# Row maxima of two early stages sent through ScalarE's own DMA queue, and a new order of the first pairs of an attention kernel

## The chip, the cores and the metric

The kernel runs on one core of one Trainium2 chip. The metric is the device time of one execution in microseconds (us), the median over several runs. TensorE is called PE, VectorE DVE, ScalarE ACT, GpSimd POOL and SyncE SP, as in the profile. SP here does nothing but issue DMAs. L531 is line 531 of the kernel.

## The reference: what is computed

Causal attention with a decay bias, four batches of eight heads, 576 positions, 64 dimensions, then two feed-forward layers on the 2304 tokens:

```python
scores = scale * np.matmul(q, k.transpose(0, 1, 3, 2))
cum = np.cumsum(np.maximum(s, 0.0), axis=-1)
bias = -(cum[:, :, :, None] - cum[:, :, None, :])
scores = np.where(causal, -1000000000.0, scores + np.minimum(bias, 0.0))
scores = scores - np.max(scores, axis=-1, keepdims=True)
attn = np.exp(scores)
attn = attn / (np.sum(attn, axis=-1, keepdims=True) + 1e-09)
out = np.matmul(attn, v)
# layer 1
h = x @ w_in
x = (h - np.tanh(h)) @ w_out
# layer 2
h = x @ w_in
x = (h * np.clip(h + 3.0, 0.0, 6.0) / 6.0) @ w_out
```

## The kernel before

**Tiling.** The 32 heads are worked as 16 pairs; all of the attention comes first (until about 185 us), then the two layers, which are long runs of matmuls and are not touched by the change. Pair 0 is split into its two heads, each with its own loads, row maxima and rows; every other pair is one unit.

**The steps of a pair p**, by the names that the planner uses (the line is that of the kernel before):
- `lq`, `lk` load q and k (L490, 288 KB each for a pair); `q1` and `k2` are copies by ACT (L466, L480), `kh` a cast by DVE (L477), `q2` a DMA from one q tile to another (`Q<-Q`, through `move`, L279), `ql` and `kl` subtractions by POOL (L474, L484), `cu` a DMA of the running sums of s.
- `mx`: PE multiplies q and k for the row maxima (L531); `rd`: DVE reduces the products (L540).
- `mf`: DVE scales, splits and transposes the maxima (L569 to L576). `mo` sends the rows to DRAM (`mdram<-xr`, 16 KB) and `mi` brings them back as two rows of the q tile (`Q<-mdram`): one round trip, two DMAs in series, both issued by SP through `move`.
- `st`: PE computes the scores in four tiles (L633), of which one operand contains the two rows that `mi` brings; `ex`: ACT's exponentials (L636); `pv`: the values and the sums (L666, L677) with v loaded by `lv` (L598); `ov`: copies out by ACT (L701).

So the scores of a head can start only when its maxima have come back from DRAM, and the planner puts the maxima of the next pairs (`mx`) between them. Where PE has nothing ready early on, **fillers** are put in (`zeros()`, L1354): matmuls of zeros into an idle PSUM bank. `FILLS` names the operation in front of which they stand and how many microseconds of them, counted at 0.115 us each. 18 wide ones (L1369) open the program.

**What sets the order.** A list-scheduling planner (`Plan`) gives every operation a planned start from the durations and due times that the code passes to it. The instructions of each engine stand in the order of these starts, and every engine runs its own in that order. `PRIO` is a table of offsets of the due times, one for each kind of step; `MOVES` then moves single operations behind others by hand. A DMA stands in the order of the engine that issues it. `first_mf` and `first_mo` list the operations `mf` and `mo` in the order head 0, head 1, pair 1, pair 2 ..., so that `first_mo[:1]` is the `mo` of the first head; operations in an `after` list wait for them in the plan alone.

`scores(h, hh, ...)` takes its rows from `omi[x]`, the `mi` of its own head or pair.

Of the kernel before, what the change touches and what calls it, by code (L numbers as in the profile page):

```python
# [23 lines left out]
NPR = NH // 2  # L24
# [6 lines left out]
ON = {}  # L31
MOVES = [("cu0b", 0, "cu0", 0), ("q2_0", 1, "lk1", 0), ("kh1", 0, "rd1_0", 0), ("mf0", 1, "rd1_2", 0)]
FILLS = {"mx1_0": 0.9, "mx2_1": 3.0, "st0_0": 0.9, "mx4_1": 2.4, "st1_0": 0.5, "pv1_3": 1.5}
NS1, NS2, NIN = 4, 2, 3
# [33 lines left out]
UMX = ((0, 1, 2, 3, 4, 5), (4, 0, 1, 3, 2))  # L68
KDMA = ()
TINY, HUGE = (float(np.array([b], np.uint32).view(np.float32)[0]) for b in (0x38000000, 0x47F00000))  # L70

# [8 lines left out]
PRIO = {  # L80
# [3 lines left out]
}  # L84
# [46 lines left out]
class Plan:  # L131
# [18 lines left out]

    def dma(self, fn, kb, after=(), bufs=(), prio=0.0, name="", n=1):
        return self.op("SP", n * self.ISSUE, fn, after, bufs, prio, kb, name)

# [6 lines left out]
    def schedule(self):  # L160
# [12 lines left out]
        while done < len(self.ops):  # L173
# [14 lines left out]
            while again:  # L188
                again = False
                for e in ready:  # L190
# [35 lines left out]
                    if e == "SP":  # L226
                        dma_free = max(dma_free, t + o.dur) + o.kb / self.DMA_KB_US
                        o.end = dma_free + self.DMA_US
                    else:
                        o.end = t + o.dur + self.LAT[e]  # L230
                    heapq.heappush(events, free[e])
# [28 lines left out]
def kernel(  # L260
# [14 lines left out]
    def f32(a):  # L275
        return a.bitcast(F32)

    def move(dst, src):
        nc.sync.dma_start(f32(dst), f32(src))  # L279

# [35 lines left out]
    def r(b):  # L316
        return late[b.t] if isinstance(b.t, str) else b.t
# [124 lines left out]
    alloc_prev = [None, None]  # L442
    first_mf, first_mo = [], []
    filled = []
# [5 lines left out]
    def heads(p):  # L450
# [10 lines left out]
        for i, a in enumerate(parts):  # L461
# [26 lines left out]
            def ld(x, a=a):  # L488
# [3 lines left out]
            lq, lk = (plan.dma(  # L492
                lambda x=x, ld=ld: ld(x), 147 * n, [cm] if p == 1 else first_mo[:1] if p == 2 else first_mo[1:2] if p else [], [tq], t + PRIO["lq"], name=f"l{'qk'[x]}{p}"
            ) for x in range(2))
# [4 lines left out]
            else:  # L499
              okh.append(plan.op("DVE", vec_us(n * S, 1.92, 150), kh, [lk, al], [b1, tq], t + PRIO["kh"], name=f"kh{p}", port=True))  # L500
              ok2.append(plan.op("ACT", act, k2, [lk, a2], [b2, tq], early(t + PRIO["k2"], 1.05), name=f"k2_{p}"))
            oq2.append(plan.dma(q2, 147 * n, [oq1[-1], a2], [b1, b2], t + PRIO["q2"], name=f"q2_{p}"))
            oql.append(plan.op("POOL", pool, ql, [oq1[-1], a2] + first_mf[: 2 * (p == 1)], [b1, b2, tq], early(t + PRIO["ql"], 2), name=f"ql{p}", port=True))
# [59 lines left out]
        for i, a in enumerate(parts):  # L563
            n = a.stop - a.start
            mr = Buf(mrp)

            def mf(a=a, n=n, mr=mr):
                if n == 2:
                    nc.vector.tensor_copy(r(mt)[0:D, 1, 4:5], r(mt)[D:P, 0, 4:5])  # L569
                m = r(mt)[:, a]  # L570
                hi, lo = (r(MT)[:, x * 5 * n : (x + 1) * 5 * n].rearrange("p (a i) -> p a i", a=n) for x in range(2))
                nc.vector.tensor_scalar_mul(hi, m, -1.0)  # L572
                nc.vector.scalar_tensor_tensor(
                    out=lo, in0=m, scalar=-1.0, in1=f32(hi), op0=ALU.mult, op1=ALU.subtract
                )
                return nc.vector.transpose(f32(r(mr)), f32(r(MT)))  # L576

            def mo(i=i, mr=mr):
                move(mdram[p if i == 0 else NPR], r(mr))

            def mi(a=a, i=i, n=n):
                rows = mdram[p if i == 0 else NPR].rearrange("(b n) r -> n b r", b=4)[0 : 10 * n]
                rows = rows.rearrange("(j n) b r -> j n b r", j=2)
                if n == 2:
                    dst = r(b1)[0][66:68].rearrange("j a (i b r) -> j (a i) b r", i=5, b=4)
                else:
                    dst = r(b1)[0][66:68, a.start].rearrange("j (i b r) -> j i b r", i=5, b=4)
                move(dst, rows)

            dep = sum((mm_mx[hh] for hh in range(a.start, a.stop)), [])  # L590
            u = t0 + PRIO["mf"] if p else lead + a.start
            omf = plan.op("DVE", 0.55 + 0.1 * n, mf, dep, [mt, MT, mr], u, name=f"mf{p}", port=True)
            omo = plan.dma(mo, 16, [omf], [mr], u, name=f"mo{p}")
            first_mo.append(omo)
            first_mf.append(omf)
            omi.append(plan.dma(mi, 5, [omo], [b1], u, name=f"mi{p}"))

        lv = plan.dma(lambda: nc.sync.dma_start(r(vf).rearrange("p j a d -> p (j a d)"), v[p]), 338, first_mo[1:2] if p else first_mo[:1], [vf], t0 + PRIO["lv"], name=f"lv{p}")  # L598
        k2s.append(ok2[-1])
# [835 lines left out]
```

## Time and profile before

| what | value |
|---|---|
| median of 3 runs | 945.47 us (944.84 to 946.5) |
| the profiled execution's own time | 944.47 us |
| its span (first to last instruction) | 942.7 us |
| mean clock granted to TensorE over the span | 0.998 of full |
| busy: PE, DVE, ACT, POOL | 931.3, 662.9, 467.3, 159.3 us |

The span is cut short of the execution's own time by 1.8 us of start and end. An engine is busy when one of its instructions runs; PE's busy time does not tell fillers from work, nor a slow clock from a fast one. A row of a timeline gives the start, the busy time of a run of equal instructions, the engine, the line, the tiles (destination, arrow, sources) and the count; in square brackets stands the idle time before it, with the work that ended it.

### The profile page before, as it was taken

To read this page: it belongs to the slowest core of one execution; us is meant where nothing else is said; L and a number is where in the kernel's file an instruction comes from. 1 tells how busy PE (TensorE), PEld (TensorE's weight loads), DVE (VectorE), ACT (ScalarE), POOL (GpSimd) and SP (SyncE) were. 2 spreads that over 40 slices of the span, in tenths; PEclk is the share of its full clock that TensorE was granted. 3 is DMA by queue.
4 is the path that set the end of the run, shared out by engine and by line. 5 is a ranking of instruction groups with operands and counts; after the bars stand their busy time and mean duration, and the time that the engine had idled before them with its cause. 6 is when DMAs were issued, how large, how long until landed. Compare 5 with 4: busy or idle time off the path is not lost.

```text
span 942.7 us, 18003 instructions
## 1 busy us (share of the span) xinstructions
PE 931.3 (99%) x7112; PEld 839.0 (89%) x7112; DVE 662.9 (70%) x1059; ACT 467.3 (50%) x720; POOL 159.3 (17%) x113
## 2 busy tenths in 40 slices
PE   8999999999999999999999999999999999999998
PEld 5888888788788889988888888999999999999997
DVE  7798897889985776676577641848767477674763
ACT  7577777655443444444344333544545344454441
POOL 7446756500000000022332321000000000000000
PEclk9999999999999999999999999999999999999999
DMA  5666876777235445564546862766887668776762
GB/s 156 170 180 176 235 197 182 229 286 233 89 121 220 179 185 217 202 202 156 216 153 223 262 218 78 261 214 222 267 276 242 212 221 267 274 245 216 223 223 92
DMA packets 69793, 193.75 MB, mean 206 GB/s; under 512 B 11856, under 2 KB 20656, under 8 KB 68428
## 3 DMA queue, kind: packets, MB, share of 16 engines
q1 hardware_dynamic: 69708, 192.59, 63.0%
q8 instruction: 56, 0.92, 0.4%
q14 instruction: 29, 0.24, 0.1%
HBM read 143.74 MB, written 44.09 MB: 199 GB/s over the span
## 4 chain that ended last, share of the span: by engine, by line
PE 91%; DVE 5%; POOL 1%; DMA 1%; issue 1%; ACT 1%; SPq 0%; DVEq 0%; POOLq 0%; ACTq 0%
PE bank L903 21%; PE bank L934 20%; PE pair L1271 19%; PE pair L1195 18%; PE bank L633 5%; PE bank L666 3%; DVE xr L540 2%; PE bank L677 2%; PE bank L531 1%; PE wide L531 1%; DMA Q<-Q 1%; PE bank L1354 1%; DVE xr L572 1%; DVE K L477 0%; POOL K L484 0%
## 5 line engine op out<-in xcount | busy, mean ns | idle before, releaser
L934 PE MATMUL bank<-gg,w 128*128 128x512 f32 (+1 forms) x960 | 234.4, 368 | 0.5 <-ACT gg L922 0.5
L903 PE MATMUL bank<-xx,w 128*128 128x512 f32 (+1 forms) x960 | 233.4, 368 | 0.0
L934 PEld LDWEIGHTS bank<-gg,w 128*128 128x128 f32 x960 | 170.4, 188 | 30.6 <-ACT gg L922 0.9
L903 PEld LDWEIGHTS bank<-xx,w 128*128 128x128 f32 x960 | 170.4, 189 | 30.2 <-issue 0.2
L1195 PE MATMUL pair<-op_w,w 128*128 128x384 f32 x648 | 117.9, 335 | 0.2
L1195 PEld LDWEIGHTS pair<-op_w,w 128*128 128x128 f32 x648 | 112.4, 188 | 1.2 <-DVE g L918 0.6
L914 ACT ACTIVATE g<-bank 128x512 f32<-128x512 f32 (+1 forms) x80 | 44.4, 555 | 136.9 <-PE bank L903 66.3
L924 POOL TENSOR_TENSOR gg<-g,gg 128x512 fp32r<-128x512 f32 x32 | 48.3, 1510 | 343.8 <-ACT gg L922 246.6
L918 DVE TENSOR_TENSOR g<-bank,g 128x512 f32<-128x512 f32 (+1 forms) x80 | 50.9, 636 | 73.5 <-ACT g L914 72.6
L1271 PE MATMUL pair<-w,op_W 128*128 128x256 f32 x774 | 97.8, 283 | 0.0
L1271 PEld LDWEIGHTS pair<-w,op_W 128*128 128x128 f32 x774 | 95.4, 192 | 0.0
L922 ACT ACTIVATE gg<-g 128x512 fp32r<-128x512 f32 (+1 forms) x80 | 47.0, 588 | 49.4 <-DVE g L918 27.4
L633 PE MATMUL bank<-Q,K 128*128 128x320 f32 (+9 forms) x384 | 65.8, 313 | 1.8 <-DMA Q<-Q 0.9
L636 ACT ACTIVATE pt<-bank 128x512 f32<-128x512 f32 (+2 forms) x128 | 59.1, 508 | 17.1 <-PE bank L633 12.0
L633 PEld LDWEIGHTS bank<-Q,K 128*128 128x128 f32 (+3 forms) x384 | 56.2, 186 | 8.1 <-issue 2.5
L1271 PE MATMUL pair<-w,op_B 128*128 128x256 f32 x486 | 62.7, 283 | 0.0
L1271 PEld LDWEIGHTS pair<-w,op_B 128*128 128x128 f32 x486 | 60.5, 192 | 0.0
L540 DVE CUSTOM_DVE_ANT_0 xr<-bank,xr 128x512 bf16<-128x512 f32 (+3 forms) x96 | 49.0, 510 | 14.5 <-PE bank L531 3.8
L474 POOL TENSOR_TENSOR Q<-tq,Q 64x1152 fp32r<-64x1152 f32 (+1 forms) x17 | 43.0, 2530 | 46.5 <-PE bank L531 22.2
L666 PE MATMUL bank<-pt,vf 128*32 128x192 f32 (+3 forms) x1152 | 46.7, 315 | 0.0
L484 POOL TENSOR_TENSOR K<-tq,K 64x1152 fp32r<-64x1152 f32 (+1 forms) x17 | 42.8, 2522 | 10.9 <-ACT Q L468 3.7
L666 PEld LDWEIGHTS bank<-pt,vf 128*32 128x32 f32 x1152 | 32.1, 110 | 11.0 <-DVE xr L540 0.6
(322 smaller groups left out, 1347.2 us busy)
## 6 DMA issues: line engine op xcount, KB each, us to landing
w<-wdram SPq DMA_DIRECT2D x149, 512.0 KB
wdram<-cv SPq DMA_DIRECT2D x56, 512.0 KB
raw_c<-in_w_dram SPq DMA_DIRECT2D x11, 1024.0 KB
raw_b<-in_w_dram SPq DMA_DIRECT2D x11, 1024.0 KB
raw_a<-in_w_dram SPq DMA_DIRECT2D x12, 512.0 KB
vf<-in_v_dram SPq DMA_DIRECT2D x16, 330.0 KB
rb<-rdram SPq DMA_DIRECT2D x32, 144.0 KB
xdram<-xb SPq DMA_DIRECT2D x16, 288.0 KB
```

What stands on the lines that cost most here:

```text
L540: nc.vector.tensor_tensor_reduce(out=junk[0:rr, 0:w], in0=r(b)[0:rr, col : col + w], in1=maskB[:, 0:w] if hh < 0 else maskA[0:rr, m0 : m0 ...
L633: nc.tensor.matmul(o, w, x, start=(i == 0), stop=(i == len(mms) - 1), skip_group_check=True)
L636: nc.scalar.activation(r(pt), r(b)[:, 0 : CW[c]], AF.Exp, scale=0.125)
L666: nc.tensor.matmul(r((wide_b, rest_b)[far])[32 * i : 32 * i + 32, oc : oc + n], r(vf)[:, j, hh, d0 : d0 + 32], r(pts[hh][c])[:, col : col ...
L903: nc.tensor.matmul(r(ps)[:, 0:w], wt[:, c, :], x(c)[:, 0:w], start=(part == 0 and c == 0), stop=(part == 2 and c == NCC - 1),)
L914: nc.scalar.activation(r(g)[:, 0:w], r(ps)[:, 0:w], AF.Tanh)
L918: nc.vector.tensor_sub(x, r(ps)[:, 0:w], x)
L922: gho = plan.op("ACT", vec_us(w, 1.2, 205), lambda: nc.scalar.activation(r(gh)[:, 0:w], r(g)[:, 0:w], AF.Copy), [m, to_gg], [g, gh], base)
L924: glo = plan.op("DVE" if beside else "POOL", vec_us(w, 0.96, 155) if beside else vec_us(w, 0.44, 160), lambda: (nc.vector if beside else n ...
L934: nc.tensor.matmul(r(acc[e])[:, 0:w], a[:, es], bb[:, 0:w], start=f, stop=l)
L1195: nc.tensor.matmul(bank(k)[:, l], w[hw][:, l, kc], r(x)[:, hx, kc], start=(i in (1, 5, 2) and j == 0 and kc == 0), stop=(j == 2 and kc == ...
L1271: nc.tensor.matmul(r(c[k])[:, m * 256 : (m + 1) * 256], r(x)[:, hx, l, m * P : (m + 1) * P], w[hw][:, l], start=(i == order[chain_first[k] ...
```

## The change

It does five things.
- `OWNQ = (1,)`: for the second head of pair 0 and for pair 1, `mo` and `mi` are issued by ACT (`nc.scalar`) in a DMA queue of its own, and not by SP. These are four DMAs.
- The planner counts a DMA issued by ACT with the landing time of a DMA.
- The loads of pair 2 (the third pair) get a due time near the start (`lead + 2`), in front of `q2_1` (`lead + 5`) and of `lv0` (`lead + 3`); `q2_1` also stands after the first head's `mo`, and the loads of the later pairs and of v wait, in the plan, for an `mf` and no longer for an `mo`.
- The table `PRIO` is new, which orders the steps of all pairs anew, and `MOVES` has two more entries, which put `mi` of the second head behind that head's exponential 1 of the first head (`ex0_1`) and `q1` of pair 2 behind `ex0_3`.
- `FILLS`: the fillers in front of pair 1's maxima (`mx2_1`) go from 3.0 to 4.4 us, those in front of the first scores go, those in front of the second head's scores go from 0.5 to 0.6, those in front of pair 2's maxima go from 2.4 to 1.2, and those in front of the first values go.

```diff
--- before.py
+++ after.py
@@ -29,8 +29,10 @@
 NEG = -8.0e9
 WARM = 18
 ON = {}
-MOVES = [("cu0b", 0, "cu0", 0), ("q2_0", 1, "lk1", 0), ("kh1", 0, "rd1_0", 0), ("mf0", 1, "rd1_2", 0)]
-FILLS = {"mx1_0": 0.9, "mx2_1": 3.0, "st0_0": 0.9, "mx4_1": 2.4, "st1_0": 0.5, "pv1_3": 1.5}
+MOVES = [
+    ("cu0b", 0, "cu0", 0), ("q2_0", 1, "lk1", 0), ("kh1", 0, "rd1_0", 0), ("mf0", 1, "rd1_2", 0), ("mi0", 1, "ex0_1", 0), ("q1_2", 0, "ex0_3", 0),
+]
+FILLS = {"mx1_0": 0.9, "mx2_1": 4.4, "st1_0": 0.6, "mx4_1": 1.2}
 NS1, NS2, NIN = 4, 2, 3
 NPT = (3, 3, 3, 3)
 PVG = ((0, 1, 2, 3),)
@@ -67,6 +69,7 @@
 ]
 UMX = ((0, 1, 2, 3, 4, 5), (4, 0, 1, 3, 2))
 KDMA = ()
+OWNQ = (1,)
 TINY, HUGE = (float(np.array([b], np.uint32).view(np.float32)[0]) for b in (0x38000000, 0x47F00000))
 
 BLOCKS = [(0, t0, w) for t0, w in ((0, 512), (512, 512), (1024, 256), (1280, 512), (1792, 512))]
@@ -78,9 +81,9 @@
 
 
 PRIO = {
-    "lq": -83.65, "q1": 73.45, "kh": -32.51, "k2": -25.57, "q2": 94.58, "ql": -115.49, "kl": 41.37, "cu": 56.98, "mx": -24.12, "rd": 29.37,
-    "mf": -136.78, "mo": -203.04, "mi": -117.08, "lv": -137.83, "st": 6.08, "ex": -106.35, "pv": 17.91, "ov": -39.21, "sd": 23.64, "so": -123.9,
-    "no": 107.64, "conv": 202.63, "T": 6.478, "dst": 0.344, "sp": 27.42, "dsp": 24.45,
+    "lq": 39.12, "q1": 73.45, "kh": -91.19, "k2": 105.65, "q2": -6.45, "ql": -64.52, "kl": 41.37, "cu": -137.68, "mx": -24.12, "rd": 129.89,
+    "mf": -136.78, "mo": 59.8, "mi": -126.96, "lv": -137.83, "st": 5.7, "ex": -84.37, "pv": 12.68, "ov": 141.74, "sd": 103.06, "so": -123.9,
+    "no": 84.45, "conv": 198.97, "T": 6.478, "dst": 0.344, "sp": 27.42, "dsp": -52.34,
 }
 
 
@@ -148,8 +151,8 @@
         self.ops.append(o)
         return o
 
-    def dma(self, fn, kb, after=(), bufs=(), prio=0.0, name="", n=1):
-        return self.op("SP", n * self.ISSUE, fn, after, bufs, prio, kb, name)
+    def dma(self, fn, kb, after=(), bufs=(), prio=0.0, name="", n=1, own=False):
+        return self.op("ACT" if own else "SP", n * self.ISSUE, fn, after, bufs, prio, kb, name)
 
     @staticmethod
     def later(ready, free, e, item, t):
@@ -227,7 +230,7 @@
                         dma_free = max(dma_free, t + o.dur) + o.kb / self.DMA_KB_US
                         o.end = dma_free + self.DMA_US
                     else:
-                        o.end = t + o.dur + self.LAT[e]
+                        o.end = t + o.dur + (self.DMA_US if o.kb else self.LAT[e])
                     heapq.heappush(events, free[e])
                     heapq.heappush(events, o.end)
                     done += 1
@@ -275,8 +278,8 @@
     def f32(a):
         return a.bitcast(F32)
 
-    def move(dst, src):
-        nc.sync.dma_start(f32(dst), f32(src))
+    def move(dst, src, own=False):
+        (nc.scalar if own else nc.sync).dma_start(f32(dst), f32(src))
 
     keep = ctx.enter_context(tc.tile_pool(name="keep", bufs=1))
     dram = ctx.enter_context(tc.tile_pool(name="dram", bufs=1, space=bass.MemoryType.DRAM))
@@ -440,7 +443,7 @@
 
     T = PRIO["T"]
     alloc_prev = [None, None]
-    first_mf, first_mo = [], []
+    first_mf, first_mo, first_mi = [], [], []
     filled = []
     st_done, pv_done, prep_done, ov_done, rd_done = {}, [], [], {}, []
     batch_sd, batch_ov, norm_ops = {}, {}, {}
@@ -490,7 +493,7 @@
                 nc.sync.dma_start(dst, (q, k)[x][p][:, a.start * S : a.stop * S])
 
             lq, lk = (plan.dma(
-                lambda x=x, ld=ld: ld(x), 147 * n, [cm] if p == 1 else first_mo[:1] if p == 2 else first_mo[1:2] if p else [], [tq], t + PRIO["lq"], name=f"l{'qk'[x]}{p}"
+                lambda x=x, ld=ld: ld(x), 147 * n, [cm] if p == 1 else first_mo[:1] if p == 2 else first_mf[1:2] if p else [], [tq], lead + 2 if p == 2 else t + PRIO["lq"], name=f"l{'qk'[x]}{p}"
             ) for x in range(2))
             oq1.append(plan.op("ACT", act + 0.22 * (p > 0), q1, [lq, al], [b1, tq], early(t + PRIO["q1"], 1), name=f"q1_{p}"))
             if p in KDMA:
@@ -499,7 +502,7 @@
             else:
               okh.append(plan.op("DVE", vec_us(n * S, 1.92, 150), kh, [lk, al], [b1, tq], t + PRIO["kh"], name=f"kh{p}", port=True))
               ok2.append(plan.op("ACT", act, k2, [lk, a2], [b2, tq], early(t + PRIO["k2"], 1.05), name=f"k2_{p}"))
-            oq2.append(plan.dma(q2, 147 * n, [oq1[-1], a2], [b1, b2], t + PRIO["q2"], name=f"q2_{p}"))
+            oq2.append(plan.dma(q2, 147 * n, [oq1[-1], a2] + first_mo[:1] * (p == 1), [b1, b2], lead + 5 if p == 1 else t + PRIO["q2"], name=f"q2_{p}"))
             oql.append(plan.op("POOL", pool, ql, [oq1[-1], a2] + first_mf[: 2 * (p == 1)], [b1, b2, tq], early(t + PRIO["ql"], 2), name=f"ql{p}", port=True))
             okl.append(plan.op("POOL", pool, kl, [ok2[-1]] + first_mf[: 2 * (p == 1)], [b2, tq], t + PRIO["kl"] if p else lead + 3.5 + 0.1 * i, name=f"kl{p}", port=True))
 
@@ -575,27 +578,30 @@
                 )
                 return nc.vector.transpose(f32(r(mr)), f32(r(MT)))
 
-            def mo(i=i, mr=mr):
-                move(mdram[p if i == 0 else NPR], r(mr))
-
-            def mi(a=a, i=i, n=n):
+            own = p + i in OWNQ
+
+            def mo(i=i, mr=mr, own=own):
+                move(mdram[p if i == 0 else NPR], r(mr), own)
+
+            def mi(a=a, i=i, n=n, own=own):
                 rows = mdram[p if i == 0 else NPR].rearrange("(b n) r -> n b r", b=4)[0 : 10 * n]
                 rows = rows.rearrange("(j n) b r -> j n b r", j=2)
                 if n == 2:
                     dst = r(b1)[0][66:68].rearrange("j a (i b r) -> j (a i) b r", i=5, b=4)
                 else:
                     dst = r(b1)[0][66:68, a.start].rearrange("j (i b r) -> j i b r", i=5, b=4)
-                move(dst, rows)
+                move(dst, rows, own)
 
             dep = sum((mm_mx[hh] for hh in range(a.start, a.stop)), [])
             u = t0 + PRIO["mf"] if p else lead + a.start
             omf = plan.op("DVE", 0.55 + 0.1 * n, mf, dep, [mt, MT, mr], u, name=f"mf{p}", port=True)
-            omo = plan.dma(mo, 16, [omf], [mr], u, name=f"mo{p}")
+            omo = plan.dma(mo, 16, [omf], [mr], u, name=f"mo{p}", own=own)
             first_mo.append(omo)
             first_mf.append(omf)
-            omi.append(plan.dma(mi, 5, [omo], [b1], u, name=f"mi{p}"))
-
-        lv = plan.dma(lambda: nc.sync.dma_start(r(vf).rearrange("p j a d -> p (j a d)"), v[p]), 338, first_mo[1:2] if p else first_mo[:1], [vf], t0 + PRIO["lv"], name=f"lv{p}")
+            omi.append(plan.dma(mi, 5, [omo], [b1], u, name=f"mi{p}", own=own))
+            first_mi.append(omi[-1])
+
+        lv = plan.dma(lambda: nc.sync.dma_start(r(vf).rearrange("p j a d -> p (j a d)"), v[p]), 338, first_mf[2:3] if p else first_mo[:1], [vf], t0 + PRIO["lv"] if p else lead + 3, name=f"lv{p}")
         k2s.append(ok2[-1])
         prep_done.extend(oq1 + okh + oql + okl + oq2 + ok2)
         bt, hp = divmod(p, NCC)
```

ACT, from the end of pair 1's copies to the exponentials of the first head. `pt_0_...` are the exponentials' tiles, `bank_70` to `bank_73` the scores of the first head, `Q_3`/`K_3` tiles of pair 3, `Q_2` those of pair 2. Before:

```order
L480 ACTIVATE K_1_111<-tq 64x2x576
L369 ACTIVATE Q_3_105<-Q_1_99 4x1280
L370 ACTIVATE K_3_106<-Q_1_99 4x2x576
L636 ACTIVATE pt_0_115<-bank_70 128x256
L636 ACTIVATE pt_0_118<-bank_71 128x320
L466 ACTIVATE Q_2_102<-tq 64x2x576
L468 ACTIVATE Q_2_104<-tq 64x64
L636 ACTIVATE pt_0_121<-bank_72 128x512
L636 ACTIVATE pt_0_124<-bank_73 128x512
```

The same place of the changed kernel:

```order
L373 ACTIVATE K_3_106<-Q_1_99 4x2x576
L282 DMA mdram<-xr 128x32
L642 ACTIVATE pt_0_115<-bank_70 128x256
L642 ACTIVATE pt_0_118<-bank_71 128x320
L282 DMA Q_0_96<-mdram 2x20x32
L642 ACTIVATE pt_0_121<-bank_72 128x512
L642 ACTIVATE pt_0_124<-bank_73 128x512
L469 ACTIVATE Q_2_102<-tq 64x2x576
L471 ACTIVATE Q_2_104<-tq 64x64
```

The second head's `mo` now stands in ACT ahead of the first exponential and its `mi` behind the second; pair 2's copy `q1` (`Q_2`) has moved behind the fourth. Pair 1's `mo` and `mi` stand likewise a little later, among the exponentials of the second head.

SP, from the first head's `mo` on (the first row in both). `Q_1_110<-Q_1_99` is `q2` of pair 1, `vf_112` v of pair 0, `K_3_106<-cdram` a `cu`. Before:

```order
L279 DMA mdram<-xr 128x32
L279 DMA Q_1_110<-Q_1_99 64x2x576
L598 DMA vf_112<-in_v_dram 128x660
L279 DMA Q_0_96<-mdram 2x20x32
L490 DMA tq<-in_q_dram 64x1152
L490 DMA tq<-in_k_dram 64x1152
L279 DMA K_3_106<-cdram 2x2x576
L279 DMA mdram<-xr 128x32
L598 DMA vf_113<-in_v_dram 128x660
L598 DMA vf_114<-in_v_dram 128x660
L279 DMA Q_0_96<-mdram 2x20x32
```

After:

```order
L282 DMA mdram<-xr 128x32
L282 DMA Q_0_96<-mdram 2x20x32
L493 DMA tq<-in_q_dram 64x1152
L493 DMA tq<-in_k_dram 64x1152
L604 DMA vf_112<-in_v_dram 128x660
L282 DMA K_3_106<-cdram 2x2x576
L282 DMA Q_1_110<-Q_1_99 64x2x576
```

The first head's `mi` has moved up to its `mo`, pair 2's loads stand ahead of v and of pair 1's `q2`, and the second head's `mo` and `mi` are gone from SP. Behind these rows stand the loads of pairs 3 and 4 and two of v. Further on, pair 2's `mi` (`Q_2_102<-mdram`) stands directly behind pair 3's `mo`:

```order
L282 DMA mdram<-xr 128x32
L282 DMA K_1_100<-cdram 2x2x576
L282 DMA Q_1_110<-Q_3_105 64x2x576
L282 DMA mdram<-xr 128x32
L282 DMA Q_2_102<-mdram 2x40x32
L282 DMA Q_3_105<-mdram 2x40x32
```

The first row is pair 2's `mo`, the fourth pair 3's; in the kernel before, pair 2's `mi` stood two rows ahead of pair 3's `mo`.

PE, in the changed kernel, at the end of the first head's scores (`bank_73`) and the start of the second head's:

```order
L639 MATMUL bank_73<-maskT,identb 128x2x128
...
L1360 MATMUL bank_70<-xr 128x256
L639 MATMUL bank_70<-Q_0_108,K_0_109 128x256
L639 MATMUL bank_70<-Q_0_96,K_0_97 128x256
L639 LDWEIGHTS identb
L639 MATMUL bank_70<-maskT,identb 128x128
L639 MATMUL bank_65<-Q_0_108,K_0_109 128x320
L639 MATMUL bank_65<-Q_0_96,K_0_97 128x320
```

Between the two scores stand five fillers, four of them and their weight loads left out here. `Q_0_108,K_0_109` is the half of the product that does not contain the rows of maxima, `Q_0_96,K_0_97` the half that does. In the kernel before stood here 20 fillers, the maxima of pair 2 and 4 fillers, and behind the second head's scores 13 fillers and then the values. In the changed kernel, the second head's scores are followed by 10 fillers, the maxima of pair 2 and the values, without fillers between the last two. The fillers in front of pair 1's maxima are 38 in place of 26; the 7 in front of the first head's scores are gone.

## Rows read from the trace of the kernel before

**Rows 1.** The page's first part: busy time, share, instructions of each engine.
```profile
PE 931.3 (99%) x7112; PEld 839.0 (89%) x7112; DVE 662.9 (70%) x1059; ACT 467.3 (50%) x720; POOL 159.3 (17%) x113
```

**Rows 2.** PE's waits over the span: us in total, times, longest us.
```profile
PE bank L531 <- DVE K L477: 1.5, 1, 1.5
...
PE bank L633 <- DMA Q<-Q: 0.9, 1, 0.9
PE bank L633 <- POOL K L484: 0.8, 1, 0.8
```

**Rows 3.** PE's timeline, 11 to 43 us.
```profile
11.27 3.01 PE L1354 MATMUL bank<-xr 128*128 128x256 bf16 x26
15.79 0.70 PE L531 MATMUL bank<-K,Q 66*128 66x512 f32 x2 [1.50 <-DVE K L477]
...
17.87 1.72 PE L1354 MATMUL bank<-xr 128*128 128x256 bf16 x7
...
24.76 1.17 PE L531 MATMUL bank<-K,Q 66*128 66x512 f32 x6 [0.48 <-issue]
...
26.68 0.61 PE L1354 MATMUL bank<-xr 128*128 128x256 bf16 x4
27.05 0.48 PE L633 MATMUL bank<-Q,K 128*128 128x256 f32 x2
...
29.05 1.58 PE L1354 MATMUL bank<-xr 128*128 128x256 bf16 x13
30.56 2.92 PE L666 MATMUL bank<-pt,vf 128*32 128x256 f32 x72
...
34.81 0.73 PE L531 MATMUL bank<-K,Q 66*128 66x512 f32 x2
...
42.41 0.45 PE L633 MATMUL bank<-Q,K 128*128 128x256 f32 x2
```

**Rows 4.** Windows: busy of PE, PEld, DVE, ACT, POOL; clock, DMA share, GB/s.
```profile
17.40:20.80 3.40, 3.40 (x17) 2.85 (x16) 2.87 (x12) 0.53 (x2) 2.67 (x2) 0.50 0.95 249
...
110.00:120.00 10.00, 10.00 (x163) 8.45 (x162) 9.13 (x28) 8.16 (x17) 5.31 (x2) 1.00 0.89 203
```

**Rows 5.** Mean granted clock of the core over its span.
```profile
core 0: 942.7 us, clock 0.998
```

**Rows 6.** DVE's timeline, 14 to 36 us.
```profile
14.93 0.76 DVE L477 CAST K<-tq 64x1152 fp32r<-64x1152 f32 x1
...
17.77 0.21 DVE L576 STREAM_TRANSPOSE xr<-xr 128x32 f32<-128x32 f32 x1
...
18.73 0.69 DVE L540 CUSTOM_DVE_ANT_0 xr<-bank,xr 128x512 bf16<-128x512 f32 x1
...
23.90 0.76 DVE L477 CAST K<-tq 64x1152 fp32r<-64x1152 f32 x1
25.27 0.69 DVE L540 CUSTOM_DVE_ANT_0 xr<-bank,xr 128x512 bf16<-128x512 f32 x1 [0.61 <-PE bank L531]
...
35.45 0.69 DVE L540 CUSTOM_DVE_ANT_0 xr<-bank,xr 128x512 bf16<-128x512 f32 x1 [1.91 <-ACT stage L701]
```

**Rows 7.** SP's queue, 13 to 23 us: start and length of each DMA issue.
```profile
13.69 0.36 SPq L279 DMA_DIRECT2D mdram<-xr  x1
...
15.53 0.79 SPq L279 DMA_DIRECT2D Q<-mdram  x1
...
18.13 0.34 SPq L279 DMA_DIRECT2D mdram<-xr  x1
...
22.02 0.69 SPq L279 DMA_DIRECT2D Q<-mdram  x1
```

**Rows 8.** ACT's timeline, 20 to 24 us.
```profile
20.18 0.38 ACT L636 ACTIVATE pt<-bank 128x256 f32<-128x256 f32 x1 [2.64 <-PE bank L633]
...
21.28 1.17 ACT L466 ACTIVATE Q<-tq 64x1152 fp32r<-64x1152 f32 x1
...
22.50 1.05 ACT L636 ACTIVATE pt<-bank 128x512 f32<-128x512 f32 x2
```

## The prediction

> **What bounds the kernel now.** First the page's busy times: PE is busy for 931.3 of 942.7 us, DVE for 662.9 [rows 1], so a gain must come out of PE's 11 us of idle time, its fillers, or a slow clock. Then PE's waits: the longest inside the work is 1.5 us, for pair 1's cast of k by DVE; two later ones are 0.9 and 0.8 us, 1.7 together [rows 2]. Then the clock: the window from 17.40 to 20.80, right behind the 1.5 us wait, has a granted clock of 0.50 (1.2 GHz), where the later window has 1.00 [rows 4]. That stretch costs 3.40 x 0.5 = 1.7 us. The mean over the span is 0.998 [rows 5], a loss of 942.7 x 0.002 = 1.9 us in all, so this is the only fall, and the waits of up to 0.9 us brought none. Last PE's timeline [rows 3]: until 34.81, when pair 3's maxima start, fillers stand between the real work, because the scores of pair 0's second head start only at 27.05. Behind that PE has no fillers. So the question is how much earlier than 34.81 PE reaches pair 3's maxima, and how much of it lasts.
>
> **The change part by part.** A filler costs 1.51/13 = 0.116 us (29.05 to 30.56 [rows 3]).
>
> *The fillers before pair 1's maxima.* The 26 run from 11.27 and PE then waits 1.50 us for the cast that ends at 14.93 + 0.76 = 15.69 [rows 3, 6]. 38 take 12 x 0.116 = 1.4 us more and cover 1.4 of the 1.50. Pair 1's maxima still start at 15.8, but no wait stands before them that could slow the clock. The 1.7 us are not added by themselves; they are part of the next sum, since they lie before 34.81.
>
> *The work up to the second head's scores.* At full clock a pair's maxima take 26.68 - 24.76 = 1.92 us, a head's scores 29.05 - 27.05 = 2.00, the values 34.81 - 30.56 = 4.25 [rows 3]. Pair 1's maxima end at 17.7, the first head's scores (no fillers before them now) at 19.7, which I set to 20.1, since their last tile goes into a bank that DVE still reads until 18.73 + 0.69 = 19.42 [rows 6]. Five fillers lead to 20.7, and the half product that needs no rows to 20.9. Then PE waits for the rows of the second head; S is the time at which its scores can go on.
>
> *S.* The second head's transpose ends at 17.77 + 0.21 = 17.98 [rows 6]. Two legs follow. Leg one, `mo` to the issue of `mi`: the trace has it at 15.53 - 13.69 = 1.84 us, where SP's queue held little, and at 22.02 - 18.13 = 3.89, where SP had issued loads ahead of it and waited [rows 7]. Leg two, from `mi`'s issue until PE goes on, has no row of its own; it is a DMA of the same kind, so I bound it by the same two. S lies between 18.0 + 2 x 1.84 = 21.7 and 18.0 + 2 x 3.89 = 25.8. In ACT's own queue nothing stands ahead of these rows, which is the situation of the first row; but the DMA engines are 95% busy from 17.40 to 20.80 [rows 4]. I take 22.0, near the low end. PE then waits 22.0 - 20.9 = 1.1 us: between the 0.9 that kept the clock and the 1.50 that lost it. I take it as kept.
>
> A rule of the Trainium skill speaks against this. "DMA: Bandwidth & Descriptors", in "Issuing engines are not separate DMA queues", says that DMAs started by different engines end up on the same 16 DMA engines, and that a second issuer saves only the issue time. By it, S would be near the upper row. The same page, in "Queues, rings and completion order", has each DMA engine turn by packets between the queues that have work, which would keep S low. No run here has shown either.
>
> *From there to pair 3's maxima.* Second head's scores 2.00, ten fillers 1.16, pair 2's maxima 1.92, values 4.25: 9.33 us. They start at S + 9.33, so the gain is 34.81 - 9.33 - S = 25.48 - S: 3.5 us at S = 22.0. It cannot exceed 4.0, since pair 2's maxima wait for a cast that ended at 23.90 + 0.76 = 24.66 [rows 6], thus S + 3.16 >= 24.66.
>
> *What ACT pays.* Four DMA issues, at SP's lengths twice 0.34 to 0.36 and twice 0.69 to 0.79 [rows 7]: 2.2 us, where ACT had an idle gap of 2.64 us in front of the first head's exponentials, waiting for PE [rows 8]; pair 1's two stand among the second head's exponentials, which wait for PE likewise. Behind the second head's `mi`, which waits for `mo`, stand two exponentials and pair 2's copy of q; the copy is wanted by pair 2's maxima at 22.0 + 3.2 = 25.2. The same work takes 22.50 + 1.05 - 21.28 = 2.3 us [rows 8], so from an issue at 19.9 and 0.7 for it, it ends at 22.9. Without the gaps the issues would cost up to 2.2 us; I take 0. *What SP gains*: it no longer waits in front of the second head's `mi`, and pair 3's loads, which stood behind it, leave earlier. `q2` of pair 1 and v of pair 0, moved behind pair 2's loads by two issues of about 0.6 us, are wanted only from 27 us on: 0.
>
> *Pair 2's rows.* Its `mi` now stands in SP behind pair 3's `mo`, so it waits for pair 3's reductions. With M the start of pair 3's maxima, PE wants it at M + (42.41 - 34.81) + 4.25 = M + 11.9, if the values of pair 1 stand where they did. Pair 3's maxima are multiplied until M + 7.6 too; a last reduction of 0.69 and a transpose of 0.21 make M + 8.5, one more reduction in arrears and the short steps around them up to M + 9.7 (an estimate), and a leg of 1.84 to 3.89 leads to M + 10.3 to M + 13.6: a wait of 0 to 1.7. I take 0; the nearer row is the short leg.
>
> *How much lasts.* The first reduction of pair 3 follows 1.91 us of DVE idle, and pair 2's 0.61 [rows 6]. DVE can thus follow PE 2.5 us earlier without new speed; later it is 91% busy [rows 4]. Of the 3.5 I take 3.5 - 2.5 = 1.0 as given back (bounds 0 and all of it). The two late waits, 1.7 us [rows 2], stand where the order is also new: -1.7 to +1.7, taken as 0.
>
> Sum: -3.5 + 1.0 = -2.5 us. The profiled 944.47 lies 1.0 under the median, so it would be 942.0 there and **943.0** on the median's scale (945.47 - 2.5).
>
> **The rivals.** A measurement of this kernel tells about 0.2%, 1.9 us.
> - *The wait before the second head's scores slows the clock.* For: at 1.1 us it is longer than any wait that kept it. Against: it is shorter than the one that lost it. Price 1.7 us: 945.47 - 2.5 + 1.7 = 944.7.
> - *The own queue does not help `mo`.* Leg one 3.89: S = 23.7, PE waits 2.8, more than 1.50, and the clock falls: gain 25.48 - 23.7 - 1.7 = 0.1, DVE gives nothing back: 945.4. For: the busy DMA engines [rows 4]. Against: the long row stood behind SP's own loads. The skill's first rule above gives this one.
> - *Slower: both legs are long.* `mi` writes rows in small pieces, which must take turns with the loads of pair 2 that now leave at the same time. S = 25.8, and with the clock 25.48 - 25.8 - 1.7 = -2.0: 947.5. It decides for slower from S = 25.7. Against: only one of the two rows is that long, and this needs both legs to be.
> - *A new late wait*: pair 2's rows 1.7 us late, or the late waits up by that: 945.47 - 2.5 + 1.7 = 944.7. For: `mi` is really behind the later `mo`. Against: it needs the long leg on a queue that has fewer issues.
>
> **How the numbers follow.** Forecast 0.52, slow clock 0.20, own queue no help 0.11, both legs long 0.09, new late wait 0.08. The forecast's own range is 945.47 - 4.0 - 1.7 = 939.8 (the largest gain, none of it given back, the late waits gone) to 944.2 (2.2 given back in place of 1.0); 0.49 of its 0.52 lie under 943.6. The two cases at 944.7 and the one at 945.4 are "same", save for 0.05 below and 0.03 above it; the long legs are slower but for 0.01. Faster 0.54, same 0.35, slower 0.11. The range leaves out one in ten at each end: 940.4 to 946.9.
>
> **What would show it.** Right: no half clock from 17 to 21 us, PE's wait at 15.8 gone, the second head's scores at about 22, pair 3's maxima near 31.3, and a wait of about 1.1 us before the scores. The middle layers start 2.5 us earlier than before. Wrong: a clock of 0.50 after 22 us (first rival), the transfer issued by ACT taking 3.9 us (second, third), a wait on `Q<-mdram` before pair 2's scores (fourth). The number is wrong, with the steps right, if the late waits move by more than a microsecond or DVE gives back more than 1.0.

## The result, and the profile after

The change makes the kernel slower: 954.75 us against 945.15 (medians of 6 runs each), a ratio of 1.0089 with an interval of 1.0066 to 1.0113. On another chip it was 1.0058 (1.0034 to 1.0082). The forecast was 943.0 in a range of 940.4 to 946.9, so it was wrong in its direction. The profiled execution took 951.96 us, with a span of 950.2 in place of 942.7 and a mean granted clock of 0.994 in place of 0.998: 7.5 us more, to be found in the profile. The ratios of this document leave out single executions of over 1500 us, of which `hold_early` had two.

PE's waits over the span (us in total, times, longest), where [rows 2] had a longest of 1.5:

```profile
PE bank L639 <- DMA Q<-mdram: 8.0, 1, 8.0
...
PE wide L534 <- ACT xb L707: 1.3, 1, 1.3
PE bank L672 <- ACT pt L642: 1.2, 1, 1.2
```

One wait of 8.0 us, for the rows of maxima on their way back. PE's timeline, against [rows 3]:

```profile
11.14 4.32 PE L1360 MATMUL bank<-xr 128*128 128x256 bf16 x38
15.79 0.70 PE L534 MATMUL bank<-K,Q 66*128 66x512 f32 x2 [0.33 <-issue]
...
20.21 0.71 PE L1360 MATMUL bank<-xr 128*128 128x256 bf16 x5
20.67 0.36 PE L639 MATMUL bank<-Q,K 128*128 128x256 f32 x1
29.06 0.58 PE L639 MATMUL bank<-Q,K 68*128 68x256 f32 x1 [8.02 <-DMA Q<-mdram]
...
32.50 2.34 PE L1360 MATMUL bank<-xr 128*128 128x256 bf16 x10
...
41.02 0.73 PE L534 MATMUL bank<-K,Q 66*128 66x512 f32 x2
```

Up to 20.67 all goes as forecast. Then the scores of the second head stand until 29.06 (S, the time at which they go on, forecast at 22.0), and pair 3's maxima start at 41.02 in place of 34.81: 6.2 of the 7.5 us. ACT's timeline tells the two legs (ACTq rows are its DMA issues), against [rows 7, 8]:

```profile
18.01 0.35 ACTq L282 DMA_DIRECT2D mdram<-xr  x1
18.41 0.71 ACT L642 ACTIVATE pt<-bank 128x256 f32<-128x256 f32 x2 [0.85 <-PE bank L639]
23.80 1.20 ACTq L282 DMA_DIRECT2D Q<-mdram  x1
25.10 1.08 ACT L642 ACTIVATE pt<-bank 128x512 f32<-128x512 f32 x2 [5.98 <-DVE K L480]
```

`mo` to `mi`'s issue is 23.80 - 18.01 = 5.79 us, `mi` to PE's start 29.06 - 23.80 = 5.26. Two exponentials stand behind `mi` for 5.98 us; the row puts this wait down to a cast of DVE's, but ACT was held by its own DMA wait. What SP issued in the meantime, at the place where it stood still until 22.02 before [rows 7]:

```profile
18.15 0.78 SPq L282 DMA_DIRECT2D Q<-Q  x1
19.02 0.55 SPq L493 DMA_DIRECT2D tq<-in_q_dram  x1
20.71 0.47 SPq L493 DMA_DIRECT2D tq<-in_k_dram  x1
22.25 0.47 SPq L493 DMA_DIRECT2D tq<-in_q_dram  x1
23.53 0.47 SPq L493 DMA_DIRECT2D tq<-in_k_dram  x1
24.05 1.65 SPq L604 DMA_DIRECT2D vf<-in_v_dram  x2
```

Seven transfers of 288 to 330 KB (pair 1's `q2`, the loads of pairs 3 and 4, two of v), one after the other, without a wait for the rows. The windows (columns as in [rows 4]) show the DMA engines full through both legs, and TensorE's clock at its lower level behind PE's idle time:

```profile
18.00:23.80 5.80, 2.94 (x21) 2.15 (x19) 5.00 (x20) 0.71 (x2) 5.25 (x2) 1.00 1.03 259
23.80:29.10 5.30, 0.04 (x1) 0.04 (x1) 0.82 (x2) 2.39 (x4) 0.00 (x0) 0.60 1.02 234
24.90:35.10 10.20, 6.04 (x26) 4.95 (x27) 0.00 (x0) 6.17 (x11) 2.62 (x1) 0.50 0.57 138
```

In the kernel before, the DMA share in the window 22.0 to 24.2, in which `mi` went, was

```profile
22.00:24.20 2.20, 2.20 (x21) 1.80 (x19) 2.02 (x9) 1.55 (x4) 1.39 (x1) 1.00 0.49 174
```

0.49. In the window of its first leg, 18.10 to 22.00, it was 0.98, so that leg (3.89) met full engines there too. So the 7.5 us are: 29.06 - 25.48 = 3.6 for the late rows (the forecast's own balance, gain = 25.48 - S), 41.02 - 29.06 - 9.33 = 2.6 for the half clock behind the wait, and a rest of 1.3 that arises later; the waits of PE behind 41.02 explain 0.9 of it (1.3, 1.2, 0.3 and 0.2 us in place of 0.9, 0.8 and 0.4).

### The profile page after: what moved, and what is told of

It is laid out like the page before. It is cut to its first block, busy times and chain, and to the rows that moved or that the text cites. A ratio compares the mean times of both kernels' runs of the same rounds, so it can differ in the third digit from the quotient of the medians.

```text
span 950.2 us, 17945 instructions
## 1 busy us (share of the span) xinstructions
PE 930.8 (98%) x7095; PEld 838.3 (88%) x7095; DVE 661.1 (70%) x1059; ACT 466.5 (49%) x720; POOL 159.6 (17%) x113
## 4 chain that ended last, share of the span: by engine, by line
PE 91%; DVE 3%; DMA 2%; ACT 1%; issue 1%; POOL 0%; SPq 0%; DVEq 0%; ACTq 0%; POOLq 0%
PE bank L909 20%; PE bank L940 20%; PE pair L1277 19%; PE pair L1201 18%; PE bank L639 5%; PE bank L672 4%; PE bank L683 2%; PE wide L534 1%; PE bank L534 1%; DMA raw_a<-in_w_dram 1%; DVE xr L543 1%; DMA Q<-mdram 1%; PE bank L1360 1%; ACT pt L642 0%; DVE K L480 0%
```

## The experiments

Three theories were set against each other. **Backlog:** SP's wait for `mo`, which the change removes, had kept SP from issuing loads; without it the loads fill the DMA engines, and the rows must pass this backlog whichever queue they are in. **Own queue:** ACT's queue is slow in itself. **Order:** the new order of steps costs the time. Each run stands beside runs of the kernel before on the same chip, to which its ratio refers.

**Undoing the own queue.** `rows_on_sp` lets the planner put the rows back on SP; `sp_same_place` leaves every step at the changed kernel's place and only changes the issuing engine.

```diff
-OWNQ = (1,)
+OWNQ = ()
```

> The changed kernel with all row DMAs issued by SP again (the new order of steps stays). If ACT's own queue is what makes the rows late: the second head's scores start at about 25 us in place of 29, the time is 944 to 947 us. If the cause is the backlog of loads that SP now issues without a stop, whatever queue the rows use: the second head's mo, which stands behind pair 1's q2, lands only at about 24.8, its mi two to four us later, the scores start at 27 to 29 and the time stays at 949 to 953. If the new order of steps itself costs the time: 952 to 955.

```diff
-        (nc.scalar if own else nc.sync).dma_start(f32(dst), f32(src))
+        nc.sync.dma_start(f32(dst), f32(src))
```

> The changed kernel word for word, but the four row DMAs are issued by SP at the places that the planner gave them (all engines keep their order, ACT loses the four issues). If the backlog is the cause and the queue hardly matters: the second head's mo, behind pair 1's q2 in SP, takes 4 to 6.5 us to land, mi stands behind pair 3's loads and takes 3 to 4 more, the scores start at 26.5 to 30 us, the time is 0.4 to 1.1% above before. If ACT's queue costs time by itself, over the backlog: the scores start at about 25, the time is within 0.3% of before.

Measured: 1.0099 (1.0065 to 1.0133) and 1.0079 (1.0049 to 1.0110). `rows_on_sp` is no clean test: the planner also put pair 2's maxima back ahead of the second head's scores, and PE stands 3.51 us in front of them, until 24.75, and never for the rows. SP's rows of `sp_same_place`, `mo` and `mi` of the second head, and PE's:

```profile
19.96 0.54 SPq L282 DMA_DIRECT2D mdram<-xr  x1
...
25.17 0.67 SPq L282 DMA_DIRECT2D Q<-mdram  x1
```

```profile
27.40 0.58 PE L639 MATMUL bank<-Q,K 68*128 68x256 f32 x1 [6.26 <-DMA Q<-mdram]
```

Leg one takes 5.21 us in SP's queue too, and S is 27.40. For the second head's rows the theory of a slow own queue falls: without it the time is no better. S is 1.7 us earlier than in the changed kernel, but a later wait, for an exponential, is 2.8 us in place of 1.2. (With the rows on SP, SP stands still from 22.1 to 25.17; the DMA share in the second leg is 0.19, and that leg, 2.23 us, is the short one there.)

**Holding the loads.** The rows stay in ACT's queue; SP issues a small DMA that reads the returned rows, and so waits for them, ahead of the loads of pair 3 (`hold_loads`) or ahead of those of pair 2 and everything behind (`hold_early`; `move(hdram, ...)` at `p == 2`, and `q2_1`, `lv0` behind it).

```diff
+    ("lq3", 0, "mi0", 1), ("lk3", 0, "lq3", 0),
 ]
...
+                if p == 3 and x == 0:
+                    move(hdram, firsts[0][0][66:68, 1, 0:S])
                 nc.sync.dma_start(dst, (q, k)[x][p][:, a.start * S : a.stop * S])
```

> The changed kernel with SP's loads of pair 3 and all that stands behind them held until the second head's rows have come back (SP issues a small DMA that reads these rows ahead of the loads, a wait that the kernel before had in another form). The rows stay in ACT's queue. If the backlog of loads is the cause: mo lands at 22 to 23.5, mi about 1.7 us after its issue, the scores start at 24.5 to 25.5, the time is 944.5 to 948. If ACT's own queue is slow by itself: mo still takes 5.4 and mi 4.0 us, the time stays at 950 to 955, or gets worse, since the loads are later too.

> The changed kernel with the rows in ACT's queue, and every load from pair 2's q on held in SP until the second head's rows are back, so that nothing is in flight when they go. If the backlog is the cause: mo to mi's issue takes 1.4 to 1.8 us in place of 5.8, mi 1.7 to 2.2, the second head's scores start at 21.3 to 22.2 us, as the prediction had it; pair 2's cast of k then comes late (its loads start only at 22: it ends at 27 to 28), so the time is about that of before or up to 4 us above. If ACT's queue is slow by itself: the legs stay at 4 and 2 us or more, the scores start at 24.5 or later.

`hold_loads` is at 1.0008 (0.9991 to 1.0025) of before: one added wait takes back nearly all of the loss. PE, DVE, ACT and POOL run in the changed kernel's order here, so the theory that this order costs the time falls with it. `mo` still had pair 2's loads, v and pair 1's `q2` ahead of it: leg one is 4.42 us, at a DMA share of 0.96. What the wait repairs is leg two, 2.17 us in place of 5.26, in a window with hardly any load:

```profile
22.40:24.60 2.20, 0.00 (x0) 0.00 (x0) 2.02 (x9) 0.86 (x2) 1.00 (x1) 0.95 0.07 14
```

S is 24.61. With `hold_early` nothing is in flight when `mo` goes. ACT's issues, and PE:

```profile
18.08 0.35 ACTq L283 DMA_DIRECT2D mdram<-xr  x1
19.64 1.20 ACTq L283 DMA_DIRECT2D Q<-mdram  x1
```

```profile
21.67 0.39 PE L643 MATMUL bank<-Q,K 68*128 68x256 f32 x1 [0.57 <-DMA Q<-mdram]
...
28.04 0.70 PE L538 MATMUL bank<-K,Q 66*128 66x512 f32 x2 [3.22 <-ACT pt L646]
```

```profile
18.00:20.80 2.80, 2.69 (x21) 2.10 (x19) 2.33 (x10) 0.71 (x2) 2.63 (x1) 1.00 0.05 9
```

With a DMA share of 0.05 the same instructions in the same queue take 1.56 and 2.03 us, and S is 21.67: the forecast's 22.0. The held loads come late in turn: PE waits 3.22 us, which the row puts down to ACT, but DVE's cast of pair 2's k ends only then, and waited for its load:

```profile
27.18 0.76 DVE L482 CAST K<-tq 64x1152 fp32r<-64x1152 f32 x1 [3.23 <-DMA tq<-in_k_dram]
```

The kernel is at 1.0025 (1.0000 to 1.0050). Backlog is shown: 5.79 and 5.26 us with full DMA engines, 1.56 and 2.03 with empty ones, by the same instructions in the same order.

**The own queue with the old tables.** `own_queue_only` is the kernel before with `OWNQ` and its code, old `PRIO`, `MOVES` and `FILLS`.

> The kernel before with nothing but ACT's own queue for the four row DMAs (its old order of steps, its old fillers). If the new order of steps is the cause: about as before, 943 to 947. If SP without the wait for the second head's mo builds up the backlog, or if the own queue is slow: the second head's scores start 2 to 5 us later than in the kernel before (27.05), the time is 948 to 953.

It is at 1.0077 (1.0046 to 1.0108), but PE's order is not the old one: with the rows in ACT's queue the planner itself puts the second head's scores ahead of pair 2's maxima. They start at 25.37, 1.7 us earlier than in the kernel before, where 2 to 5 us later was expected. PE waits 3.9 us for the rows, the clock falls, and 20 fillers stand behind:

```profile
15.79 0.70 PE L532 MATMUL bank<-K,Q 66*128 66x512 f32 x2 [1.65 <-DVE K L478]
...
25.37 0.58 PE L636 MATMUL bank<-Q,K 68*128 68x256 f32 x1 [3.87 <-DMA Q<-mdram]
...
28.81 3.92 PE L1357 MATMUL bank<-xr 128*128 128x256 bf16 x20
```

So a loss does not need the new tables, but this run does not tell how much of its own loss the backlog makes. Its legs are 4.43 and 2.93 us, at DMA shares of 0.91 and 0.62. It shows something else: PE waits 1.65 us before pair 1's maxima, where the kernel before waited 1.50, and the clock behind it stays at 1.00:

```profile
15.80:25.20 9.40, 5.56 (x38) 4.64 (x38) 7.74 (x30) 3.91 (x7) 5.62 (x5) 1.00 0.83 209
```

**The price of the clock.** `fill_8` keeps PE busy while it waits.

```diff
-FILLS = {"mx1_0": 0.9, "mx2_1": 4.4, "st1_0": 0.6, "mx4_1": 1.2}
+FILLS = {"mx1_0": 0.9, "mx2_1": 4.4, "st1_0": 8.4, "mx4_1": 1.2}
```

> The changed kernel with 8.4 us of fillers before the second head's scores in place of 0.6. The rows are as late as before, but PE is busy while it waits. If about 3 us of the loss are the slow clock behind the 8 us wait: no granted clock of 0.5 after 29 us, the scores and pair 2's maxima run at their full-speed lengths, and the time falls by 2.5 to 3.5 us. If the clock does not matter there (PE would wait again for the exponentials and DVE): less than 1 us.

```profile
20.94 8.78 PE L1360 MATMUL bank<-xr 128*128 128x256 bf16 x73
29.47 0.49 PE L639 MATMUL bank<-Q,K 128*128 128x256 f32 x2
...
38.70 0.74 PE L534 MATMUL bank<-K,Q 66*128 66x512 f32 x2
```

Pair 3's maxima start 2.3 us earlier than in the changed kernel, and the span is 947.0 in place of 950.2; the ratio to before is 1.0028 (1.0006 to 1.0050). The rows are earlier in this execution (`mi` is issued at 21.98, and PE does not wait for them), but the fillers keep the scores until 29.47, no earlier than the 29.06 of the changed kernel. From there to pair 3's maxima are 9.23 us in place of 11.96, so nearly 3 us of the loss were the half clock. `changed_again` is the changed kernel on a second chip, with a 6.9 us wait at the same place; its ratio, 1.0058, lies under the 0.7% expected:

> The changed kernel once more, on one chip with the next two, as their measure. Backlog theory: mo to mi's issue again 5 us or more, a half clock of 7 us or more behind PE's wait, 0.7 to 1.1% above before.

**Can the forecast's gain be had?** `hold_fill` is `hold_loads` with 4.2 us of fillers before the second head's scores and none before pair 2's maxima; `sp_held` the same with the rows on SP (`mo`, then `mi`, both ahead of pair 1's `q2`); `hold_fill_all` has 4.6, 1.2 and, before the first values, 1.5 us of fillers.

> The kernel with SP's later loads held (hold_loads), with 4.2 us of fillers in front of the second head's scores in place of 0.6 and none in front of pair 2's maxima. If the slow clock behind the wait was what was left of the loss there: no half clock behind 24.6, pair 3's maxima start at 32.5 to 33.5 us (34.81 in the kernel before, 36.81 in hold_loads), the time is 2 to 4 us under hold_loads, 0.1 to 0.4% under before. If a gain at this place is given back later by DVE: within 0.1% of before.

> As hold_fill, but the rows go through SP again: mo in front of pair 1's q2, mi right behind mo, so that SP's own wait for mo holds the loads. If ACT's queue has no worth of its own: the second head's scores start at 24 to 25 us as with the own queue, and the time is that of hold_fill within 0.15%. If the own queue has a gain that the backlog hid: 1 us or more slower than hold_fill.

> As hold_fill (rows in ACT's queue, later loads held), but with fillers also in front of pair 2's maxima (1.2 us) and of the first values (1.5), and 0.4 more before the second head's scores, so that no wait of over a microsecond is left until pair 3's maxima. If hold_fill's median of 951 came from a clock that falls at its waits of 1.2 and 1.7 us in most executions: the clock is at 0.996 or more in most of them, the time is within 0.2% of before, and the 2.5 us that pair 3's maxima came earlier there is gone into fillers. If the time goes elsewhere: still 0.3% or more above before.

`hold_fill`'s profiled execution (span 943.4, clock 0.999) has pair 3's maxima at 32.28, 2.5 us earlier than before, as the balance says, and then:

```profile
32.28 0.73 PE L538 MATMUL bank<-K,Q 66*128 66x512 f32 x2
34.72 1.10 PE L538 MATMUL wide<-K,Q 66*128 66x512 f32 x5 [1.71 <-DVE xr L547]
```

```profile
PE wide L538 <- ACT xb L711: 1.4, 1, 1.4
...
PE bank L676 <- ACT pt L646: 1.2, 1, 1.2
```

DVE is not ready for the next tile, and part of the reason is the hold itself: DVE waits for a k whose load SP issued only behind the rows.

```profile
32.42 0.76 DVE L482 CAST K<-tq 64x1152 fp32r<-64x1152 f32 x1 [1.18 <-DMA tq<-in_k_dram]
```

The 2.5 us are gone by the end of the span, and 0.7 more. Over its executions `hold_fill` took from 943.68 us at a clock of 0.999 to 957.73 at 0.987, at 1.0044 (1.0015 to 1.0072) of before: ten of twelve had a clock of 0.992 or less. That their clock fell at these waits is likely, but not shown.

`sp_held`, 1.0079 (1.0050 to 1.0107), is 3.6 us slower than `hold_fill` on the same chip, where its expectation asked for 1 us to show a gain of ACT's queue. The second head's rows do not make it: S is 24.81, with 0.34 us of wait. It comes at pair 1's rows, which go through SP here as well. Among the loads of the later pairs their legs are 5.62 and 6.03 us, at DMA shares of 1.03 and 1.06, PE waits for them, and the 12 us behind are at half clock; in `hold_fill` they leave at 25.11 in ACT's queue, in place of 26.97 behind SP's loads, and PE did not wait for them. So for pair 1's rows ACT's queue is worth something.

```profile
32.59 0.68 SPq L283 DMA_DIRECT2D Q<-mdram  x1
```

```profile
38.62 0.58 PE L640 MATMUL bank<-Q,K 68*128 68x256 f32 x1 [2.19 <-DMA Q<-mdram]
```

```profile
38.00:50.00 12.00, 11.38 (x52) 9.55 (x56) 5.81 (x22) 7.64 (x13) 4.75 (x2) 0.50 0.41 86
```

`hold_fill_all` gives 1.0023 (1.0006 to 1.0039). Its profiled execution kept a clock of 1.000 and still has a span of 945.2: the first leg was 5.44 us in it, S 25.65, pair 3's maxima at 36.20. The expectation of 0.2% was just missed, and only three of its twelve executions had the clock of 0.996 that the expectation asks of most. So the waits of 1.2 and 1.7 us are not all that lowers it; one of 1.4 us, for a copy of ACT's behind pair 3's maxima, is left in its profile.

**The fillers alone.** `fills_only` is the kernel before with 38 fillers in place of 26 before pair 1's maxima; `fills_two` has, in addition, 33 in place of 20 before pair 2's.

```diff
-FILLS = {"mx1_0": 0.9, "mx2_1": 3.0, "st0_0": 0.9, "mx4_1": 2.4, "st1_0": 0.5, "pv1_3": 1.5}
+FILLS = {"mx1_0": 0.9, "mx2_1": 4.4, "st0_0": 0.9, "mx4_1": 3.8, "st1_0": 0.5, "pv1_3": 1.5}
```

> The kernel before with one number changed: 4.4 us of fillers in place of 3.0 before pair 1's maxima (26 become 38), as in the changed kernel. If a wait of 1.5 us there is what halves the clock: no half clock at 17.4. If the half clock there cost PE time, as the prediction counted: about 1.7 us faster, 0.2%. If the slow stretch is hidden by the fillers and by the wait for pair 2's cast behind it: pair 2's maxima start at 24.7 as before, no change within 0.1%.

> The kernel before with rows on SP and its old order, and two fillers longer: 4.4 us in place of 3.0 before pair 1's maxima and 3.8 in place of 2.4 before pair 2's, so that neither the wait of 1.5 us at 15.8 nor the one of 1.6 us at 24.8 (fills_only) is left. If the clock of the kernel before falls at these waits in the executions that take longer than 945 us: most executions have a clock of 0.998 or more, the time is 0.1 to 0.4% under before. If it falls elsewhere (the later waits of 0.9 us): within 0.1% of before. The profiled start of pair 3's maxima stays at 34.8 in both cases.

`fills_only` has no half clock in its profile, and PE gets to the next wait earlier and waits there:

```profile
15.79 0.70 PE L531 MATMUL bank<-K,Q 66*128 66x512 f32 x2 [0.36 <-ACT K L480]
...
24.76 1.18 PE L531 MATMUL bank<-K,Q 66*128 66x512 f32 x6 [1.64 <-ACT pt L636]
...
34.80 0.73 PE L531 MATMUL bank<-K,Q 66*128 66x512 f32 x2
```

Pair 3's maxima start at 34.80 in place of 34.81, and the kernel is no faster: 1.0022 (1.0005 to 1.0039), where a change within 0.1% was expected. `fills_two` covers that wait too, with PE again at 34.83:

```profile
20.99 3.77 PE L1354 MATMUL bank<-xr 128*128 128x256 bf16 x33
...
34.83 0.73 PE L531 MATMUL bank<-K,Q 66*128 66x512 f32 x2
```

It is at 0.9977 (0.9957 to 0.9998) of before, 944.42 us against 946.76: a gain that is just clear of none, on one chip. Its 12 executions lie between 943.95 and 947.63, with clocks of 0.996 to 1.000, those of the kernel before on that chip between 943.81 and 952.10, with clocks of 0.990 to 0.998. The fastest are alike; what it gains is a clock that falls less often.

## Why the prediction was wrong

- **Fillers and the work up to the scores: right.** The 38 fillers left a wait of 0.33 us, the clock stayed at 1.00 until 24.9, and the half product ended at 20.67 + 0.36 = 21.0 (forecast 20.9). That the 1.7 us must not be counted by themselves was right: `fills_only` got nothing for them.
- **The step that failed: S.** "S lies between 21.7 and 25.8", from legs of 1.84 to 3.89 us; measured 29.06, legs of 5.79 and 5.26. Neither row that I took as a bound holds for the changed kernel. In the short one SP issued two other DMAs between the legs and did not wait for `mo` at all, at a DMA share of 0.12 (13.7 to 15.5); the changed kernel, whose first `mi` stands right behind `mo`, has 1.45 there. The long one met full engines already (0.98); behind it SP's own wait for `mo` held the next loads back, so that the second leg met a share of 0.49. I saw that wait, and counted its end as a gain of SP's ("pair 3's loads, which stood behind it, leave earlier"), at nothing. Under it lay the cause: what leaves earlier collides with the rows. This is worst for leg two, which I bounded by rows of leg one: 5.26 us at a share of 1.02, 2.0 to 2.2 at 0.02 to 0.19 (`hold_early`, `hold_loads`, `hold_fill_all`, `sp_same_place`). I chose the low end because ACT's queue has nothing ahead of the rows; `hold_early` shows this value, 21.67, for empty DMA engines, and the share of 0.95 [rows 4] spoke against them being empty. The slower rival named the right mechanism (loads that now leave at the same time; it meant pair 2's, and those of pairs 3 and 4 and of v did it), but with legs of 3.89 us, and got 0.09.
- **The clock.** The first rival's 1.7 us was the size of the one fall in the kernel before. With an 8 us wait the clock was at half for 10.2 us, 6.0 of them behind the wait, at a cost of 2.6 before pair 3's maxima. The bounds that I took for a fall, 0.9 us that kept the clock and 1.50 that lost it, do not hold from run to run: waits of 1.65 (`own_queue_only`, the same place), 1.64 (`fills_only`) and 1.71 us (`hold_fill`) kept it at 1.00 in their profiles, and in `fill_8`'s it was at half in the window 18.9 to 22.2, with no wait of PE over 0.3 us between 10.3 and there.
- **S + 9.33 to pair 3's maxima: right** where the clock holds, save that 9.33 counts the half product before S a second time (0.1 to 0.2 us). `hold_fill` started the scores at 24.07, had no fillers behind (8.17 us in place of 9.33) and reached them at 32.28; 24.07 + 8.17 = 32.24.
- **How much lasts: mis-sized, as far as is known.** I gave back 1.0 of 3.5 us. `hold_fill` came 2.5 early at pair 3's maxima and ended 0.7 late: 3.2 given back, part of it to loads that the hold delays. So no run has the rows in time without a cost for it, and whether the forecast's gain would have lasted stays open; `hold_early`, with S at 21.67, and `hold_fill` both ended at or above the time of before.
- **ACT's issues, SP's moves at 0:** no wait in the changed kernel's profile names them up to 41.02, where the rows cover all else, so they are not tested. The late wait on pair 2's rows came in no profile of these runs.
- **Open:** `fills_only` is at 1.0022 though its profile is as short as before; which of its executions lose the clock where, one profile cannot tell. Nor is it settled what, besides long waits, lowers the clock in single executions, as in `fill_8`'s window:

```profile
18.90:22.20 3.30, 3.30 (x16) 2.61 (x16) 2.80 (x11) 0.21 (x1) 3.22 (x2) 0.50 1.00 236
```

By the Trainium skill, "DMA: Bandwidth & Descriptors", "Issuing engines are not separate DMA queues", a second issuing engine saves issue time alone. `sp_same_place` and `hold_early` agree for the second head's rows: with full engines leg one was 5.21 us by SP and 5.79 by ACT, with empty ones 1.56 by ACT.

## What to carry to other kernels

A wait in an in-order DMA queue also holds back what stands behind it. Before a small transfer is moved out of such a queue, ask what the queue will now send in its place, and price the transfer by what is in flight when it goes as well as by what stands ahead of it in its queue; a small DMA that waits for the transfer's result, put ahead of the loads, restores the hold. Where PE must wait for several microseconds, price the clock behind the wait too: soon behind the waits of 2.2 to 8.0 us named here it was at half. Fillers can be worth it even where they move no work forward (`fills_two`), but need not be (`fills_only`).

## What the runs showed that I had not expected

A queue with little work got no early turn. In the changed kernel ACT's queue (q10) moved nothing between the end of `mo`'s issue and 20.1, while SP's (q1) kept the engines full (packets, MB, share of 16 engines, for the windows 18.4 to 20.1 and 20.1 to 22.9):

```profile
q1 hardware_dynamic: 121, 0.38, 101.6%
...
q1 hardware_dynamic: 305, 0.76, 101.8%
q10 hardware_dynamic: 144, 0.02, 4.3%
```

For `mi` it was the same from 25.0 to 27.5. The Trainium skill, in the same page's "Queues, rings and completion order", has each engine turn between queues packet by packet. The trace does not contradict it, but a turn is far from immediate here: 1.7 us for `mo`'s and 2.5 for `mi`'s first packet, where `hold_early`, with empty engines, had about 0.5 and 0.3. `mi`'s 42 packets then went within 0.3 us; of `mo`'s 144 packets nine came only behind 22.6, more than a microsecond after the others, and `mi`, which waits for all of them, was issued at 23.80.

And the spread between executions of one kernel goes with the clock: `hold_fill` took 943.68 us at 0.999 and 956.41 at 0.988.
